# Longer bursts of the probability-value products in one part of an attention and Fourier-mixing kernel, with casts, loads and a transpose put elsewhere

## The chip, the core and the metric

The kernel runs on one core of a Trainium2 chip. The metric is device microseconds of the whole program. The engines are named as the profile names them: PE (TensorE, matmuls), PEld (its weight loads, which run beside the matmuls), DVE (VectorE), ACT (ScalarE), POOL (GpSimd) and SP (SyncE, which here only issues DMAs).

## What is computed

Two blocks over 2048 tokens of width 640 are mixed by a gate. Block A is attention with 32 heads of 20 elements; block B is a Fourier transform along the width and then along the sequence, of which the real part is kept.

```python
g = sigmoid((x * gate_w).sum(-1, keepdims=True))
q, k, v = split_heads(x @ wqkv)                  # 32 heads of 20
p = softmax(einsum("bhqd,bhkd->bhqk", q, k) * 20 ** -0.5)
a = merge_heads(einsum("bhqk,bhkd->bhqd", p, v)) @ wo
re, im = xB @ dft_hid_re.T, xB @ dft_hid_im.T
b = dft_seq_re @ re - dft_seq_im @ im
out = g * a + (1 - g) * b
```

All operands are fp32. A product that must be exact is made of three fp32r products of parts: an operand is cast to fp32r (its first part), and what the cast left out is its second part.

## The kernel before, in words

**Stages.** First come projections of q, k and v (lines 399 to 463). Then the attention runs for 1024 *steps*; beside it PE is given other matmuls as *fills*. There are 32 units (a pair of heads and half of the queries), each of 32 steps. The fills are, in this order: the rest of the Fourier transform along the width (the hidden part, 56 cycles), the transform along the sequence (the sequence part, 168 cycles), and the output projection (the output part, 32 cycles).

**A cycle** is four steps and follows a string of letters, `ORDERS` (lines 36 to 40):

- `e` is one score matmul (L907, 62 rows deep, 512 columns) with keys on the output's partitions. ACT turns it into probabilities by an exp (L909) into a tile `p`. There are 8 in a cycle.
- `m` is one score matmul (L187) with queries on the partitions, for a later unit, 41 steps ahead. DVE takes its maximum (L189). There are 8 in a cycle. When a unit's 64 maxima columns are there, DVE makes a negated maximum `nm` of them (L203), PE transposes it (L221), DVE splits the result into two fp32r parts (L114, L115), and SP writes them as two more rows beside q, so that the later `e` matmuls subtract the maximum.
- `F` is a place for fills. One fill of the sequence part (L608) is two matmuls of 64 rows and 320 columns, one on each half of the array's rows.
- `B` is the burst (function `burst`, L913): `av_step` for two key tiles. One key tile is four matmuls (L528), each of 21 output columns, on four column groups side by side, fp32, which the profile counts as two each. So a burst is 16 matmul records in four groups of four.

An `e` or `m` matmul uses half of the array's rows. The two tuples behind each string say which half comes first, so that both halves get the same work.

**Banks.** Of PSUM's eight banks, five (`ps0` to `ps4`) are taken in turn by scores and by the transpose, one is `av`, in which a unit's 16 key tiles are summed, and two are `yp0` and `yp1` for the fills. A score can't start before the bank of the score five places before it has been read. `av` is copied out by ACT at a unit's end (L536).

**What sets the order.** The program is written out by hand: each engine executes its instructions in the order in which this code calls them, and waits only for data and buffers. DMAs and slower steps hang on step numbers (`at_step`, `begin`).

**Operands of the sequence part.** Per 16 sequence tiles (48 fills, three cycles), two tiles `part` of Fourier coefficients are made: loaded by SP (L495), for some products summed of two (L501, POOL), cast (L114, POOL) and the remainder taken (L115, POOL). Of the transform along the width, 16 tiles `x` are made for each of seven products: loaded to `araw` (L512), for some products summed (L517, POOL), cast and subtracted on POOL (L114, L115). `run_extras` in the burst issues these, some bursts after the load. When 16 sequence tiles are done, ACT reads one half of the result (L627), DVE adds the other (L628), and POOL adds it to what was there (L742).

Of the kernel before, what the change touches and what calls it, by code (L numbers as in the profile page):

```python
# [75 lines left out]
def mix_kernel(ctx: ExitStack, tc: tile.TileContext, xa, wqk, wb, cdft, wo, out):  # L76
# [12 lines left out]
    ps_a = pools(name="ps_a", bufs=1, space=PSUM)  # L89
# [32 lines left out]
    turn = itertools.count()  # L122

    def bank():
        return ps_w.tile([P, 512], F32, name=f"ps{next(turn) % 5}")

    def pair_tile():
        return work.tile([P, 2, 512], F32, name="p", bufs=5)
# [4 lines left out]
    def part_tile():  # L133
        return work.tile([P, 2, 1024], R, name="part", bufs=3)

    def v_tile():
        return work.tile([P, NS, VW], F32, name="v", bufs=2)
# [102 lines left out]
    av = ps_a.tile([P, 512], F32, name="av")  # L240
    dve.memset(av, 0.0)
# [5 lines left out]
    def load_v(n):  # L247
# [5 lines left out]
        sp.dma_start(vts[n], v_scr[p])  # L253
# [10 lines left out]
    def load_first():  # L264
        wr, w = raw_tile()[:, : ND * P].rearrange("p (d c) -> p d c", d=ND), part_tile()
        w = w.rearrange("p z c -> p (z c)")[:, : 2 * ND * P].rearrange("p (z d c) -> p z d c", z=2, d=ND)
# [11 lines left out]
        split(w[:, 0, :1], w[:, 1, :1], wr[:, :1], act, dve)  # L278
        for d in range(ND):
            if d == 1:  # L280
                split(w[:, 0, 1:], w[:, 1, 1:], wr[:, 1:], act, dve)
            split(xs[0][:, 0, d], xs[0][:, 1, d], xr[d][1], act, dve)

    def load_wqk(c):
# [3 lines left out]
        def finish():  # L288
            w = part_tile().rearrange("p z c -> p (z c)")[:, : 2 * ND * P].rearrange("p (z d c) -> p z d c", z=2, d=ND)
            split(w[:, 0], w[:, 1], raw, act, dve)  # L290
# [26 lines left out]
    def qk_tile(c, t):  # L317
        w = wt[c]
        ps = bank()
        for d in range(ND):  # L320
            three(ps, w[:, 0, d], w[:, 1, d], xs[t][:, 0, d], xs[t][:, 1, d], d == 0, d == ND - 1)
# [13 lines left out]
    def v_pair(hf, s):  # L335
        vst = v_tile().rearrange("p s e -> p (s e)").rearrange("p (a k e) -> p a k e", a=NP // 2, k=2)
# [151 lines left out]
    def load_c(g):  # L488
# [9 lines left out]
        def finish():  # L498
            c = cparts[g] = part_tile()
            if len(raws) > 1:  # L500
                pool.tensor_tensor(raws[0], raws[0], raws[1], op=ALU.add if PRODUCTS[n][0][1][0] > 0 else ALU.subtract)  # L501
            split(c[:, 0], c[:, 1], raws[0], pool, pool)

        return finish

    def load_a(n, s):
# [7 lines left out]
        def finish():  # L514
            a = a_tile(n % 2, s)
            if len(raws) > 1:
                pool.tensor_tensor(raws[0], raws[0], raws[1], op=ALU.add if PRODUCTS[n][1][1][0] > 0 else ALU.subtract)  # L517
            split(a[:, 0], a[:, 1], raws[0], pool, pool)
# [531 lines left out]
```

## Time and profile before

Three runs took 1867.81, 1868.01 and 1868.48 us (median 1868.01 us). The profiled execution took 1869.47 us by the same clock; its span, from the first to the last instruction of the profile, was 1867.7 us, and shares and sums below go by this span.

| stage, us of the span | length | PE busy | DVE | ACT | POOL | DMA share |
|---|---|---|---|---|---|---|
| projections, 0 to 260 | 260 | 256.4 | 88.4 | 73.3 | 108.9 | 0.53 |
| hidden part, 260 to 606 | 346 | 345.7 | 277.4 | 276.7 | 98.3 | 0.28 |
| sequence part, 606 to 1668 | 1062 | 1062.0 | 891.2 | 768.0 | 853.4 | 0.58 |
| output part and tail, 1668 to 1868 | 200 | 194.3 | 126.7 | 154.1 | 102.0 | 0.28 |

The columns are the engines' busy time in each stage. A busy PE is one with a matmul in flight; several can be in flight at once, on different rows or columns of the array, so this column can't tell a dense stage from a loose one. What does is the distance in time from the start of one matmul to the next on the same half of the array. The granted TensorE clock was 0.99 to 1.00 in all four stages.

### The profile page before, as it was taken

What the parts mean: (1) busy time and instruction counts of PE and PEld (TensorE: products, weight loads), DVE (VectorE), ACT (ScalarE), POOL (GpSimd) and SP (SyncE); (2) the same over time, 40 slices, a digit from 0 to 9 for tenths busy, and PEclk for the clock granted to TensorE, in tenths of its full rate; (3) what the DMA queues carried; (4) which work ended last, traced back from release to release, by engine and by line L of the source; (5) the groups of instructions that cost most, each with busy time, mean ns of one, the idle gap of its engine ahead of it and who ended that gap; (6) DMA issues with size and microseconds to landing.
All of it is one profiled execution on the core that took longest, in us unless ns stands there. A gap on an engine that the chain in (4) does not pass through costs nothing.

```text
span 1867.7 us, 45004 instructions
## 1 busy us (share of the span) xinstructions
PE 1858.3 (100%) x17606; PEld 1360.8 (73%) x17606; DVE 1383.7 (74%) x2310; ACT 1272.1 (68%) x2439; POOL 1162.6 (62%) x1038
## 2 busy tenths in 40 slices
PE   9999999999999999999999999999999999999998
PEld 8988777676767777777777777767777777776666
DVE  3044458787878888888888888888888888888853
ACT  4222258787877777777777777777777777778885
POOL 3335432121146897466799899867779989635544
PEclk9999999999999999999999999999999999999999
DMA  6744341222134674535567576546476766431233
GB/s 230 174 136 151 139 127 56 78 65 68 54 99 139 209 209 142 161 128 175 185 192 241 163 249 191 176 140 179 145 240 203 214 198 202 142 90 47 88 98 108
DMA packets 178771, 281.61 MB, mean 151 GB/s; under 512 B 44811, under 2 KB 113547, under 8 KB 178559
## 3 DMA queue, kind: packets, MB, share of 16 engines
q1 hardware_dynamic: 177599, 276.77, 47.4%
q0 software_dynamic: 960, 1.97, 0.6%
q8 instruction: 138, 2.26, 0.5%
q14 instruction: 74, 0.61, 0.1%
HBM read 214.61 MB, written 63.52 MB: 149 GB/s over the span
## 4 chain that ended last, share of the span: by engine, by line
PE 98%; DMA 1%; POOL 0%; ACT 0%; DVE 0%; issue 0%; SPq 0%; POOLq 0%; ACTq 0%
PE av L528 25%; PE yp L608 19%; PE ps L907 16%; PE ps L187 15%; PE yp L363 7%; PE ps L118 4%; PE ps L120 4%; PE ps L119 4%; PE yp L715 3%; PE ps L221 0%; DMA p<-in_xa 0%; POOL p L115 0%; DMA a_scr<-raw 0%; DVE mx L189 0%; ACT p L323 0%
## 5 line engine op out<-in xcount | busy, mean ns | idle before, releaser
L189 DVE TENSOR_REDUCE mx<-ps 128x1 f32<-128x512 f32 x2048 | 1280.1, 684 | 298.9 <-PE ps L187 280.7
L909 ACT ACTIVATE p<-ps 128x512 f32<-128x512 f32 x2048 | 1109.1, 599 | 371.6 <-PE ps L187 248.9
L187 PE MATMUL ps<-kst,qst 60*128 60x512 f32 x1920 | 758.3, 410 | 0.0
L907 PE MATMUL ps<-qst,kst 62*128 62x512 f32 x1920 | 744.9, 407 | 0.1
L608 PE MATMUL yp<-x,part 64*128 64x320 f32 x5376 | 662.1, 306 | 0.3 <-ACT raw L373 0.3
L608 PEld LDWEIGHTS yp<-x,part 64*128 64x128 f32 x5376 | 624.7, 186 | 8.3 <-ACT raw L373 0.6
L528 PE MATMUL av<-p,v 128*21 128x512 f32 x4096 | 490.1, 596 | 0.0
L907 PEld LDWEIGHTS ps<-qst,kst 62*128 62x128 f32 x1920 | 348.1, 185 | 182.5 <-DVE mx L189 132.2
L187 PEld LDWEIGHTS ps<-kst,qst 60*128 60x128 f32 x1920 | 342.2, 184 | 7.9 <-issue 4.2
L115 POOL TENSOR_TENSOR part<-raw,part 128x1024 fp32r<-128x1024 f32 (+1 forms) x128 | 288.0, 2250 | 10.3
L528 PEld LDWEIGHTS av<-p,v 128*21 128x21 f32 x4096 | 97.6, 100 | 221.5 <-issue 218.3
L363 PE MATMUL yp<-wb,x 64*128 64x320 f32 x1920 | 224.0, 307 | 0.0
L374 POOL TENSOR_TENSOR raw<-raw 128x320 f32<-128x320 f32 x64 | 55.7, 870 | 268.4 <-ACT raw L373 219.1
L363 PEld LDWEIGHTS yp<-wb,x 64*128 64x128 f32 x1920 | 210.1, 186 | 6.0
L114 POOL CAST part<-raw 128x1024 fp32r<-128x1024 f32 (+1 forms) x128 | 126.1, 985 | 127.9 <-PE ps L187 67.0
L501 POOL TENSOR_TENSOR raw<-raw,raw 128x1024 f32<-128x1024 f32 x77 | 185.9, 2414 | 7.5 <-DMA raw<-in_cdft 6.0
L115 POOL TENSOR_TENSOR x<-araw,x 128x320 fp32r<-128x320 f32 x112 | 97.8, 873 | 9.0
L715 PE MATMUL yp<-x,part 64*128 64x320 f32 x768 | 102.2, 308 | 0.0
L323 ACT ACTIVATE p<-ps 128x512 f32<-128x512 f32 x40 | 23.8, 597 | 102.0 <-PE ps L120 85.5
L715 PEld LDWEIGHTS yp<-x,part 64*128 64x128 f32 x768 | 92.0, 186 | 1.0
L118 PE MATMUL ps<-x,part 128*128 128x512 f32 x200 | 80.7, 403 | 1.6 <-ACT x L112 1.3
L114 POOL CAST p<-p 128x512 fp32r<-128x512 f32 x40 | 24.7, 618 | 92.4 <-ACT p L323 92.4
(110 smaller groups left out, 1419.5 us busy)
## 6 DMA issues: line engine op xcount, KB each, us to landing
raw<-in_cdft SPq DMA_DIRECT2D x192, 512.0 KB
araw<-a_scr SPq DMA_DIRECT2D x192, 160.0 KB
qk_scr<-p SPq DMA_DIRECT2D x40, 512.0 KB
kst<-qk_scr SPq DMA_DIRECT2D x84, 160.0 KB
qst<-qk_scr SPq DMA_DIRECT2D x84, 160.0 KB
yt<-y_scr SPq DMA_DIRECT2D x80, 160.0 KB
a_scr<-raw SPq DMA_DIRECT2D x64, 160.0 KB
y_scr<-yt SPq DMA_DIRECT2D x64, 160.0 KB
```

What stands on the lines that cost most here:

```text
L114: e1.tensor_copy(dst1, src)
L115: e2.tensor_tensor(dst2, src, f32(dst1), op=ALU.subtract)
L118: pe.matmul(ps, st1, mv1, start=first, stop=False)
L187: pe.matmul(ps, q[b : b + KROWS, qt * P : (qt + 1) * P], k[b : b + KROWS, kc * 512 : (kc + 1) * 512], start=True, stop=True)
L189: return lambda: dve.tensor_reduce(mx[n][:, h, qt, kc : kc + 1], ps, axis=AX.X, op=ALU.max)
L363: pe.matmul(yp[h][:, :HE], x[r, xz, d, cs], w[r, wz, d, :HE], start=d == 0 and z == 0, stop=d == ND - 1 and z == 2)
L501: pool.tensor_tensor(raws[0], raws[0], raws[1], op=ALU.add if PRODUCTS[n][0][1][0] > 0 else ALU.subtract)
L528: pe.matmul(av[32 * j : 32 * j + DH + 1, :], v[:, kt, h * (DH + 1) : (h + 1) * (DH + 1)], pp[qc][:, h, :], start=kt == 0, stop=kt == NS - 1)
L608: pe.matmul(yp[h][:, :HE], c[r, cz, cs], a[r, az], start=s == 0 and z == 0, stop=s == NS - 1 and z == 2)
L715: pe.matmul(yp[h][:, :HE], o[oz][r], wos[d, hf][r, wz], start=d == 0 and z == 0, stop=end)
L907: pe.matmul(pt, k[b : b + KROWS + 2, kt * P : (kt + 1) * P], q[b : b + KROWS + 2, qc * 512 : (qc + 1) * 512], start=True, stop=True)
L909: act.activation(pts[n, kt, qc][:, h], pt, AF.Exp, scale=float(DH) ** -0.5)
```

## The change

In the sequence part alone, a cycle becomes six steps: 12 `e`, 12 `m`, 24 fills in 18 places, and a burst of three key tiles. So there are 112 cycles in place of 168; the hidden and the output part keep theirs. The new string packs the scores and the fills otherwise. With it come:

- 16 key tiles are no multiple of 3, so a unit can end inside a burst. Then the next unit takes another bank: all six banks are in one queue `places`, `av` is one of them, and `next_av` puts the old one at the queue's end. Scores still have five in turn.
- An `av` matmul is 32 columns wide in place of 21 (the 11 others reach into the next head's columns, and their results are not used), so each `v` tile has 16 zeroed columns behind it (POOL).
- The cast of `part` and of `x` goes from POOL to ACT in this part, and is issued by `run_casts` in the burst; the loads of `araw` and the sums of two are issued in the middle of the cycle (`run_loads`).
- The transpose of the maxima stands ahead of the burst's last key tile in this part; before, it stood behind the burst.
- Buffers: seven `p` tiles in place of five, two `part` tiles in place of three.

```diff
 ORDERS = (
     ("ememFFFeFFmeFFmFeFmFeFmFmFFeFemB", (0, 0, 1, 0), (1, 1, 0, 1)),
+    ("ememeFFFFmeFFemFeFmFemFeFeFmeFFmeFFFFmmemmB", (0, 0, 0, 1, 0, 1), (1, 1, 0, 1, 0, 0)),
+    ("emFeFmFeFFmFeFFmeFFmeFFmFmFeFmeB", (1, 0, 1, 1), (0, 1, 0, 0)),
     ("emFFeFmFeFFmFeFmFeFFmeFmFFmFemeB", (0, 1, 1, 0), (1, 0, 0, 1)),
-    ("emFeFmFeFFmFeFFmeFFmeFFmFmFeFmeB", (1, 0, 1, 1), (0, 1, 0, 0)),
 )
...
-    turn = itertools.count()
+    places = collections.deque(f"ps{k}" for k in range(6))
+
+    def place_tile(name):
+        return ps_w.tile([P, 512], F32, name=name)
 
     def bank():
-        return ps_w.tile([P, 512], F32, name=f"ps{next(turn) % 5}")
+        places.rotate(-1)
+        return place_tile(places[-1])
...
-    av = ps_a.tile([P, 512], F32, name="av")
-    dve.memset(av, 0.0)
+    av = {"name": places.pop()}
+
+    def next_av():
+        places.append(av["name"])
+        av["name"] = places.popleft()
+        av["tile"] = place_tile(av["name"])
+
+    av["tile"] = place_tile(av["name"])
...
-        def finish():
-            a = a_tile(n % 2, s)
+        def combine():
             if len(raws) > 1:
                 pool.tensor_tensor(raws[0], raws[0], raws[1], op=ALU.add if PRODUCTS[n][1][1][0] > 0 else ALU.subtract)
-            split(a[:, 0], a[:, 1], raws[0], pool, pool)
-
-        return finish
-
-    def av_step(i, n, kt):
+
+        def parts(e1):
+            a = a_tile(n % 2, s)
+            split(a[:, 0], a[:, 1], raws[0], e1, pool)
+
+        return combine, parts
+
+    def av_step(i, n, kt, split_unit):
         v = vts[n]
+        if split_unit:
+            next_av()
+        t, c0 = av["tile"], kt * VW
         pp = [pts.pop((n, kt, qc)) for qc in range(2)]
         for qc in range(2):
             for h in range(2):
                 j = 2 * qc + h
-                pe.matmul(av[32 * j : 32 * j + DH + 1, :], v[:, kt, h * (DH + 1) : (h + 1) * (DH + 1)],
+                pe.matmul(t[32 * j : 32 * j + 32, :], v[:, c0 + h * (DH + 1) : c0 + h * (DH + 1) + 32],
                           pp[qc][:, h, :], start=kt == 0, stop=kt == NS - 1)
...
-        if s % 8 == 4 and cfin and g // 8 + 2 < 2 * UNITS:
-            cfin.pop(0)()
+        if s % 8 == 2 and g // 8 + 2 < 2 * UNITS:
+            cfin[0][0]()
...
-        if more(g):
-            n = g // (HT * NS) + 1
-            preps.append(load_a(n, made.setdefault(n, 0)))
-            made[n] += 1
-        if len(preps) > 2 or preps and not more(g):
-            preps.pop(0)()
...
+    def run_casts():
+        if cfin and (done - HIDS) // 24 + 1 < 2 * UNITS:
+            cfin.pop(0)[1](act)
+        while preps["combined"]:
+            preps["combined"].pop(0)[1](act)
+
+    def run_loads(c):
+        while preps["loaded"]:
+            preps["combined"].append(preps["loaded"].pop(0))
+            preps["combined"][-1][0]()
+        n = c // (2 * HT) + 1
+        if n < len(PRODUCTS):
+            k = made.get(n, 0)
+            made[n] = min(NS, k + 1 + (c % 4 == 3))
+            preps["loaded"].extend(load_a(n, s) for s in range(k, made[n]))
...
-        edge.append(edge[-1] + 3)
+        edge.append(edge[-1] + 2)
...
     def burst(c):
         for n in ends:
             max_nm(n)
-        run_extras(max(done - HIDS, 0) // 3, 2)
-        for kt in (2 * c, 2 * c + 1):
-            av_step(now[0], kt // NS, kt % NS)
+        k, _, i = phase(c)
+        steps = 6 if k == 1 else 4
+        run_extras(steps - 2)
+        if k == 1:
+            run_casts()
+        for kt in range(i // 2, (i + steps) // 2):
+            if k == 1 and ends and kt == (i + steps) // 2 - 1:
+                max_chain(ends.pop(0))
+            av_step(now[0], kt // NS, kt % NS, kt % NS == 0 and kt > i // 2)
         while ends:
             max_chain(ends.pop(0))
...
+            if k == 1 and x == len(order) // 2:
+                run_loads(c - HID)
```

PE's order around a burst of the sequence part that has a transpose. Before, from the last fill of a cycle to the first fill of the next (L608 is a fill, L907 an `e`, L187 an `m`, L528 the burst, L221 the transpose):

```order
L608 MATMUL yp_17233<-x_14678,part 128x320
L608 MATMUL yp_17234<-x_14678,part 128x320
L907 MATMUL ps_17423<-qst_91,kst_89 128x512
L187 MATMUL ps_17426<-kst_90,qst_92 128x512
L907 MATMUL ps_17429<-qst_91,kst_89 128x512
L528 MATMUL av<-p,v 21x512 x8
L221 MATMUL ps_17449<-ident,nm 16x128
L907 MATMUL ps_17456<-qst_91,kst_89 128x512
L187 MATMUL ps_17459<-kst_90,qst_92 128x512
L608 MATMUL yp_17233<-x_14678,part 128x320
```

The same place with the change, from the cycle's last scores (L950 is an `e`, L197 an `m`, L556 the burst, L231 the transpose, and `ps_16895` is the bank that serves as `av`):

```order
L197 MATMUL ps_17366<-kst_87,qst_89 128x512
L950 MATMUL ps_17369<-qst_88,kst_86 128x512
L197 MATMUL ps_17372<-kst_87,qst_89 128x512
L197 MATMUL ps_17375<-kst_87,qst_89 128x512
L556 MATMUL ps_16895<-p,v 32x512 x8
L231 MATMUL ps_17398<-ident,nm 16x128
L556 MATMUL ps_16895<-p,v 32x512 x4
L950 MATMUL ps_17409<-qst_88,kst_86 128x512
L197 MATMUL ps_17413<-kst_87,qst_89 128x512
L950 MATMUL ps_17416<-qst_88,kst_86 128x512
L197 MATMUL ps_17419<-kst_87,qst_89 128x512
L950 MATMUL ps_17427<-qst_88,kst_86 128x512
```

The transpose has moved from behind the burst to between its second and third key tile; before, `e`, `m`, `e` stood last ahead of a burst and two scores behind it ahead of the next fill; now `m`, `m`, `e`, `m`, `m` stand ahead (the first of them just above these rows) and five scores behind.

ACT's order around a burst of the sequence part, before (L909 is an exp, L627 the read of a fills' result):

```order
L909 ACTIVATE p<-ps_14895 128x512
L909 ACTIVATE p<-ps_14901 128x512
L627 ACTIVATE m<-yp_14586 128x320
L909 ACTIVATE p<-ps_14922 128x512
L909 ACTIVATE p<-ps_14938 128x512
```

and with the change (L952 is an exp, L113 a cast):

```order
L952 ACTIVATE p<-ps_17348 128x512
L952 ACTIVATE p<-ps_17369 128x512
L113 ACTIVATE part<-raw 128x1024
L113 ACTIVATE x_17385<-araw 128x320 x2
L952 ACTIVATE p<-ps_17409 128x512
L952 ACTIVATE p<-ps_17416 128x512
```

One cast of a whole `part` and one or two of an `x` tile now stand between the last exp of a cycle and the first of the next.

More of the change, by code (lines that the diff above doesn't have):

```diff
@@ L133, in part_tile, with w_tiles @@
     def part_tile():
-        return work.tile([P, 2, 1024], R, name="part", bufs=3)
+        return work.tile([P, 2, 1024], R, name="part", bufs=2)
+    def w_tiles():
+        w = part_tile()
+        return [w[:, z, : ND * P].rearrange("p (d c) -> p d c", d=ND) for z in range(2)]
     def v_tile():
-        return work.tile([P, NS, VW], F32, name="v", bufs=2)
+        return work.tile([P, NS * VW + 16], F32, name="v", bufs=2)
     def load_part(t, o, p, parts, blocks):
@@ L807, in mix_kernel @@
             share = count * (c + 1 - c0) // (c1 - c0) - count * (c - c0) // (c1 - c0)
-            places = order_of(c)[0].count("F")
-            goals[c] = [at_goal + share * (f + 1) // places for f in range(places)]
+            fills_ = order_of(c)[0].count("F")
+            goals[c] = [at_goal + share * (f + 1) // fills_ for f in range(fills_)]
             at_goal += share
@@ L953, in take @@
             pool.tensor_tensor(y, y, m, op=ALU.add)
-    ring = itertools.cycle([(ps_w, f"ps{k}") for k in range(5)] + [(ps_a, "av"), (ps_y, "yp0"), (ps_y, "yp1")])
+    ring = itertools.cycle([(ps_w, name) for name in (*places, av["name"])] + [(ps_y, "yp0"), (ps_y, "yp1")])
     def free_bank():
```

83 lines of the change are left out of this document (47 added, 36 removed).

## The prediction

> **What bounds the kernel now.** I read the page first, then the timeline of PE in the sequence part, then DVE's, ACT's and POOL's rows against it.
>
> ```profile
> span 1867.7 us, 45004 instructions
> PE 98%; DMA 1%; POOL 0%; ACT 0%; DVE 0%; issue 0%; SPq 0%; POOLq 0%; ACTq 0%
> ```
>
> The second line is the chain that ended last, by engine: PE is all of it. So only what makes PE's starts lie farther apart or closer counts. One whole cycle of the sequence part in the timeline (start, duration, engine, line, output<-inputs, count):
>
> ```profile
> 904.71 1.92 PE L528 MATMUL av<-p,v 128*21 128x512 f32 x16
> 905.16 0.12 PEld L528 LDWEIGHTS av<-p,v 128*21 128x21 f32 x4 [0.31 <-issue]
> 905.59 0.12 PEld L528 LDWEIGHTS av<-p,v 128*21 128x21 f32 x4 [0.31 <-issue]
> 906.56 0.50 PE L907 MATMUL ps<-qst,kst 62*128 62x512 f32 x1
> 906.56 0.50 PE L187 MATMUL ps<-kst,qst 60*128 60x512 f32 x1
> 906.90 0.60 PE L608 MATMUL yp<-x,part 64*128 64x320 f32 x5
> 907.20 0.40 PE L907 MATMUL ps<-qst,kst 62*128 62x512 f32 x1
> 907.34 0.39 PE L187 MATMUL ps<-kst,qst 60*128 60x512 f32 x1
> 907.44 0.31 PE L608 MATMUL yp<-x,part 64*128 64x320 f32 x1
> ...
> 910.68 0.39 PE L907 MATMUL ps<-qst,kst 62*128 62x512 f32 x1
> 911.00 1.91 PE L528 MATMUL av<-p,v 128*21 128x512 f32 x16
> ```
>
> A cycle is 911.00 - 904.71 = 6.29 us: a burst of 906.56 - 904.71 = 1.85 and a stretch of scores and fills of 911.00 - 906.56 = 4.44. A score holds its half of the array for 907.44 - 907.20 = 0.24 us (the fill at 907.44 follows the `e` at 907.20 on the same half; the `m` at 907.34 runs on the other). With eight scores and sixteen fills for each half, and 0.18 of edges (below), a fill takes (4.44 - 0.18 - 8 x 0.235) / 16 = 0.148. A group of four burst matmuls takes 905.59 - 905.16 = 0.43.
>
> **Fewer changes between bursts and scores: a gain.** Three edges of a cycle cost more than the work in it. The first two scores hold their halves 906.90 - 906.56 = 0.34, which is 0.10 over 0.24. The last score's start and the burst's lie 911.00 - 910.68 = 0.32 apart, 0.08 over. The burst's four groups are 1.72 of its 1.85, 0.13 over. That is 0.31 us for a cycle, however long its burst. Twelve scores and 24 fills on each half and six groups are exactly one and a half times the old contents, so the new cycle would last 1.5 x (6.29 - 0.31) + 0.31 = 9.28 us. With 112 in place of 168, 56 x 0.31 = **-17.4 us**.
>
> **The transpose ahead of the last key tile: a loss.** DVE makes `nm` behind all maxima of the cycle. How that stands to PE in a burst of before:
>
> ```profile
> 891.96 1.91 PE L528 MATMUL av<-p,v 128*21 128x512 f32 x16
> 892.44 0.68 DVE L189 TENSOR_REDUCE mx<-ps 128x1 f32<-128x512 f32 x1
> 893.04 0.21 DVE L203 TENSOR_REDUCE nm<-mx 128x16 f32<-128x64 f32 x1
> 893.80 0.28 PE L221 MATMUL ps<-ident,nm 128*16 128x128 f32 x1
> 894.01 0.50 PE L907 MATMUL ps<-qst,kst 62*128 62x512 f32 x1
> ...
> 907.13 5.06 DVE L189 TENSOR_REDUCE mx<-ps 128x1 f32<-128x512 f32 x8 [0.56 <-PE ps L187]
> L221 PE MATMUL ps<-ident,nm 128*16 128x128 f32 x21 | 5.8, 277 | 0.0
> ```
>
> `nm` is there at 893.04 + 0.21 = 893.25, 1.29 behind the burst's start; PE comes to the transpose at 893.80, 1.84 behind it. So nobody waits, and the transpose costs 894.01 - 891.96 = 2.05 less 1.85 = 0.20. After the change PE is at the transpose after two key tiles again, thus at 1.84, but DVE is later. The string ends in `m m e m m`: by 0.235 for each score on a half, and 0.32 for the last, these four `m` start 0.79, 0.55, 0.32 and 0.32 ahead of the burst. A reduction starts 0.47 behind its score (907.13 against the `m` of 906.56, less the 0.10 of a first pair) and the next 0.60 later (893.04 - 892.44). So DVE starts them at -0.32, 0.28, 0.88 and 1.48 from the burst's start, `nm` at 2.08, and has it at 2.29. PE waits 2.29 + 0.05 - 1.84 = 0.50. Besides, PE drains ahead of the transpose (893.80 is 0.12 more than four groups behind 891.96), spends 894.01 - 893.80 = 0.21 on it, and only then does the last key tile. That is 0.8 for a transpose, 0.6 more than before, in 21 bursts of this part (the count in the last row): **+12.8 us**. Below, with no wait, this is 21 x 0.1 = 2; above, with 0.2 more for a DVE that also ends late, 17. I take the worked value. What is queued behind the wait is the burst's last key tile and all scores of the next cycle; ACT and DVE then run empty, which gives nothing back.
>
> **Packed scores and five banks: a loss.** A score needs the bank of the score five places before it. In the output part before, fills are few and scores dense:
>
> ```profile
> 321.64 0.63 PE L528 MATMUL av<-p,v 128*21 128x512 f32 x4
> 327.81 0.63 PE L528 MATMUL av<-p,v 128*21 128x512 f32 x4
> ...
> 1680.23 0.63 PE L528 MATMUL av<-p,v 128*21 128x512 f32 x4
> 1686.23 0.63 PE L528 MATMUL av<-p,v 128*21 128x512 f32 x4
> 1688.66 0.60 ACT L909 ACTIVATE p<-ps 128x512 f32<-128x512 f32 x1 [0.81 <-PE ps L187]
> 1689.32 0.18 PEld L187 LDWEIGHTS ps<-kst,qst 60*128 60x128 f32 x1
> 1689.32 0.49 PE L187 MATMUL ps<-kst,qst 60*128 60x512 f32 x1
> ```
>
> There the exp ends at 1689.26, the weights of the score that gets its bank load 0.06 later, and the score lasts 0.49 in place of 0.39: a bank comes back 0.16 behind its reader's end. A cycle there has twelve fills: 12 x 0.148 + 8 x 0.235 + 0.31 + 1.72 = 5.69, but the starts lie 1686.23 - 1680.23 = 6.00 apart; the banks cost 0.31. In the hidden part (fifteen fills, the first two rows) it is 6.17 against 6.13, 0.04. In the sequence part it is nothing. By scores that is 0.229 us of work for each score in the output part, 0.256 in the hidden part, 0.266 in the sequence part (fills and scores of a half, over sixteen). The new string has 0.266 as a mean, but between its two clumps of fills fourteen scores share thirteen fills: 7 x 0.235 + 13 x 0.148 = 3.57, which is 0.255, the hidden part's density. That gives 14/16 of 0.04, and the sixth score, behind five at once and five fills, adds some 0.03: its bank's exp starts 0.57 and ends 1.17 behind the cycle's start, so it is back at 1.33, and its half is free at 0.34 + 0.235 + 5 x 0.148 = 1.31. I take 0.07 for a cycle, **+7.8 us**; the bounds are 0 and the output part's 0.31 x 24/16 = 0.47, so 0 to 52 us. It is nearest to the hidden part.
>
> **32 columns for 21: a small loss.** A weight load grows with its columns:
>
> ```profile
> L907 PEld LDWEIGHTS ps<-qst,kst 62*128 62x128 f32 x1920 | 348.1, 185 | 182.5 <-DVE mx L189 132.2
> L528 PEld LDWEIGHTS av<-p,v 128*21 128x21 f32 x4096 | 97.6, 100 | 221.5 <-issue 218.3
> ```
>
> That is (185 - 100) / 107 = 0.8 ns for a column, 9 ns for eleven. Only the first load of a burst lies open (the 0.08 ahead of it is about its length); the others run under the group before. 200 bursts x 9 ns: **+1.8 us**, bounds 0 and 2.
>
> **Casts on ACT, loads and sums in mid-cycle, buffers: nothing.** What hides them is a whole cycle: a `part` is cast a cycle ahead of its first fill, an `x` up to sixteen cycles. POOL loses the two casts and gets the small memset of `v` for each new pair of heads. Without that cover each late tile would stop PE for its lateness. What ACT must not do is hold the exps up:
>
> ```profile
> 904.62 1.09 ACT L909 ACTIVATE p<-ps 128x512 f32<-128x512 f32 x2 [0.39 <-PE yp L608]
> 905.60 0.44 ACT L627 ACTIVATE m<-yp 128x320 f32<-128x320 f32 x1
> L112 ACT ACTIVATE x<-raw 128x1024 fp32r<-128x1024 f32 x6 | 6.4, 1062 | 9.3 <-DMA raw<-in_xa 9.3
> L112 ACT ACTIVATE x<-raw 128x512 fp32r<-128x512 f32 x4 | 2.5, 623 | 2.1 <-DMA raw<-in_xa 2.1
> L112 ACT ACTIVATE p<-o 128x256 fp32r<-128x256 f32 x2 | 0.8, 418 | 1.2 <-DVE o L1006 1.2
> ```
>
> Two exps take 1.09, so the second adds 0.49 to 0.60. The new string's last `e` starts 0.55 ahead of the burst and its exp ends some 0.5 behind the burst's start; the next cycle's first exp is due 0.6 behind its first score, that is 2.58 + 0.13 + 0.6 = 3.3 behind. In these 2.8 us stand one cast of 1024 columns (1.06), one or two of 320 (0.42 to 0.62 each by the rows, I take 0.47), and at times the read (0.44) or the copy of `av` (as long as an exp, 0.60): 1.5 to 2.6. It fits, so I take nothing; below there is no gain, since PE waited for none of POOL's casts; above it is the second rival.
>
> **Sum.** -17.4 + 12.8 + 7.8 + 1.8 = +5.0 us on the profiled span of 1867.7. The median of the runs, 1868.0, is within 0.3 of that span, so I add the sum to it: **1873 us**, slower by 0.27%. The two large losses are each less sure than the gain; the likeliest case's own range is 1869 to 1879.
>
> **Rivals.**
>
> *The gain comes through (faster).* If `nm` is there when PE comes, and the banks keep up, what is left is -17.4 + 2 + 1.8 = -13.6: **1854 us**. For it: in every burst shown DVE was done 0.55 ahead of PE. Against: that was with one `m` in the last 0.5 us ahead of the burst, not three. Chance 0.22.
>
> *ACT's casts hold the exps up (slower).* The cast of `x` waits for POOL's sum, issued in mid-cycle, and ACT can't pass it. Such a stop exists in the trace, where the hidden part ends:
>
> ```profile
> 602.57 0.50 PE L907 MATMUL ps<-qst,kst 62*128 62x512 f32 x1
> 602.89 0.77 ACT L373 ACTIVATE raw<-yp 128x320 f32<-128x320 f32 x2 [1.32 <-DMA a_scr<-raw]
> 604.02 0.62 ACT L909 ACTIVATE p<-ps 128x512 f32<-128x512 f32 x1
> ...
> L115 POOL TENSOR_TENSOR part<-raw,part 128x1024 fp32r<-128x1024 f32 x110 | 262.6, 2388 | 8.8
> L501 POOL TENSOR_TENSOR raw<-raw,raw 128x1024 f32<-128x1024 f32 x77 | 185.9, 2414 | 7.5 <-DMA raw<-in_cdft 6.0 <-PE ps L187 1.5
> L517 POOL TENSOR_TENSOR araw<-araw 128x320 f32<-128x320 f32 x80 | 69.9, 874 | 0.7 <-DMA araw<-a_scr 0.7
> ```
>
> ACT waited for a DMA, and an exp came 604.02 - 602.57 = 1.45 behind its score in place of 0.6. The Trainium skill, "PSUM — Partial Sum Buffer", section "Engine vs sequencer instructions", states that ScalarE's queue is strict FIFO; that is this rival's rule, and these rows agree with it. POOL's work in a cycle with all sums is 2.39 + 2.41, two to four of 0.87 for `x`, and on average one more of that shape for a result: 9.2 at most against 9.35, and 7.6 on average with five tiles `x` in four cycles. So for some cycles the sum for `x` ends close to ACT's turn. It decides from 0.3 us of lateness on; with 0.2 us lost in each cycle the forecast rises by 112 x 0.2 = 22 to **1895 us**. Chance 0.16.
>
> *It cancels.* With the transpose's wait as worked out and no loss at the banks: -17.4 + 12.8 + 1.8 = -2.8, **1865 us**; that the casts and loads do nothing at all is part of this and of the forecast. Chance 0.14.
>
> **How the numbers follow.** The forecast has 0.48, the rivals 0.22, 0.16 and 0.14. What a measurement can't tell from no change is 0.2%, 3.7 us. Faster than that is the first rival and a little of the third: 0.24. Within it are most of the third and the forecast's lower end (1869 to 1871.7): 0.18. Slower are the rest of the forecast and the second rival: 0.58. The range, 1854 to 1892, holds all but the far half of each outer rival.
>
> **What will show it.** In the sequence part, bursts start some 9.35 us apart: 9.28 would say that the banks cost nothing, 9.5 that they cost more. Burst edges stay at 0.34, 0.32 and 0.13. In bursts with a transpose, `nm` ends 2.3 us behind the burst's start and PE starts the transpose right behind it, the cycle being 0.8 longer; a transpose at 1.84 refutes that step. First exps behind a burst that start over 0.7 behind their score would mean the second rival, as would PE waiting on ACT with a cast ahead. A wait of PE for `part` or `x` would refute the cover.

## The result, and the profile after

The changed kernel took 1879.03 us (median of 4 runs, 1877.31 to 1881.32) against 1867.91 before: a ratio of 1.006, 95% interval 1.0042 to 1.0077. The forecast was 1873, slower. Two of the versions below had one run each of another length, 8134.42 and 3615.46 us, which their ratios leave out. The profiled execution has a span of 1877.5 us against 1867.7, so 9.8 us are to be found. The page, its first line and the chain that ended last, by engine:

```profile
span 1877.5 us, 44813 instructions
PE 95%; DVE 3%; issue 0%; DMA 0%; POOL 0%; ACT 0%; SPq 0%; POOLq 0%; ACTq 0%; DVEq 0%
```

The chain was 98% PE and 0% DVE before; now 3% of it is DVE, some 56 us. In each burst of the sequence part that has a transpose the chain leaves PE for the last four maxima and `nm` (2.6 us around the burst at 641.24). That is the length of DVE's pieces in the chain and not PE's idle time, which is shown below. In the same profile the distances between bursts tell in which stage the time came: to the first burst +2.0 us, hidden part +1.0, sequence part to the first output burst +6.2, output part +0.7, tail -0.1. One plain cycle of the sequence part, PE's timeline of the changed kernel (start, duration, engine, line, operation):

```profile
765.02 0.43 PE L197 MATMUL ps<-kst,qst 60*128 60x512 f32 x2
765.38 2.78 PE L556 MATMUL ps<-p,v 128*32 128x512 f32 x24
768.09 0.50 PE L950 MATMUL ps<-qst,kst 62*128 62x512 f32 x1
768.09 0.73 PE L197 MATMUL ps<-kst,qst 60*128 60x512 f32 x2
768.43 0.63 PE L950 MATMUL ps<-qst,kst 62*128 62x512 f32 x2
...
774.71 2.78 PE L556 MATMUL ps<-p,v 128*32 128x512 f32 x24
```

The cycle is 774.71 - 765.38 = 9.33 long (median of the 90 plain cycles 9.344, forecast 9.35). The burst is 768.09 - 765.38 = 2.71, which is six groups of 0.43 and the same 0.13 as before; the first pair of scores holds its halves 768.43 - 768.09 = 0.34, again as before. So an edge costs what it cost, and there are fewer of them. The third edge is unchanged too: the last score's start and the burst's lie 0.32 apart (median in both kernels). A burst with a transpose, all engines:

```profile
641.24 1.92 PE L556 MATMUL ps<-p,v 128*32 128x512 f32 x16
...
643.28 0.21 DVE L213 TENSOR_REDUCE nm<-mx 128x16 f32<-128x64 f32 x1
643.54 0.09 PEld L231 LDWEIGHTS ps<-ident,nm 128*16 128x16 f32 x1 [1.29 <-DVE nm L213]
643.55 0.28 PE L231 MATMUL ps<-ident,nm 128*16 128x128 f32 x1 [0.38 <-DVE nm L213]
643.75 1.06 PE L556 MATMUL ps<-p,v 128*32 128x512 f32 x8
644.75 0.50 PE L950 MATMUL ps<-qst,kst 62*128 62x512 f32 x1
...
651.38 1.07 PE L556 MATMUL ps<-p,v 128*32 128x512 f32 x8
```

`nm` ends 643.28 + 0.21 - 641.24 = 2.25 behind the burst's start (forecast 2.29), the transpose starts at 2.31, and the cycle lasts 651.38 - 641.24 = 10.14. In 14 of the 21 such bursts it is so; in the other seven `nm` ends at 2.38 to 2.41, and the cycle is 0.1 to 0.2 longer still. The table of waits of PE's matmuls in this kernel (who, for whom: us in all, times, longest), its first row and one that the kernel before does not have:

```profile
PE ps L231 <- DVE nm L213: 9.3, 22, 0.5
...
PE ps L197 <- ACT p L952: 1.2, 1, 1.2
```

The first row stands 22 times in the profile where the kernel before has one such wait of 0.4. The second is a single event, late in the sequence part; POOL, ACT and PE of the changed kernel around it:

```profile
1588.09 0.46 POOL L115 CAST x<-raw 128x320 fp32r<-128x320 f32 x1 [4.21 <-DMA raw<-in_wo]
...
1594.01 2.38 POOL L516 TENSOR_TENSOR raw<-raw,raw 128x1024 f32<-128x1024 f32 x1
1596.42 1.06 ACT L113 ACTIVATE part<-raw 128x1024 fp32r<-128x1024 f32 x1 [3.23 <-POOL raw L516]
1597.39 5.47 ACT L952 ACTIVATE p<-ps 128x512 f32<-128x512 f32 x11
1598.02 0.50 PE L197 MATMUL ps<-x 60*128 60x512 f32 x1 [1.21 <-ACT p L952]
```

POOL stood 4.21 us for a load of output weights, so its sum for `part` came late; ACT stood 3.23 us in front of the cast of `part`, the exps queued behind it, and the score that needed a bank of theirs started 1.21 late. The cycle is 1.6 longer than its like. That is the mechanism of the second rival (it named the cast of `x`, here it is that of `part`), in one cycle of 112. The Trainium skill, "PSUM — Partial Sum Buffer", section "Engine vs sequencer instructions", calls ScalarE's queue strict FIFO, and these rows agree.

The five banks can be seen in the plain cycle above. Its sixth score takes the bank of its first `e`; ACT reads that one, and the score's weights follow:

```profile
768.69 0.60 ACT L952 ACTIVATE p<-ps 128x512 f32<-128x512 f32 x1 [1.89 <-PE ps L197]
...
769.34 0.18 PEld L197 LDWEIGHTS ps<-kst,qst 60*128 60x128 f32 x1
```

The exp ends at 769.29, and the weights load 0.05 behind it, as they do in the median of the plain cycles. So this score waits for its bank, where the forecast put a loss.

### The profile page after: what moved, and what is told of

Its sections match the earlier page's. It is cut to its first block, busy times and chain, and to the rows that moved or that the text cites. A ratio compares the mean times of both kernels' runs of the same rounds, so it can differ in the third digit from the quotient of the medians.

```text
span 1877.5 us, 44813 instructions
## 1 busy us (share of the span) xinstructions
PE 1858.4 (99%) x17606; PEld 1372.2 (73%) x17606; DVE 1380.5 (74%) x2309; ACT 1355.7 (72%) x2645; POOL 1002.0 (53%) x851
## 4 chain that ended last, share of the span: by engine, by line
PE 95%; DVE 3%; issue 0%; DMA 0%; POOL 0%; ACT 0%; SPq 0%; POOLq 0%; ACTq 0%; DVEq 0%
PE ps L556 23%; PE yp L636 19%; PE ps L950 17%; PE ps L197 14%; PE yp L379 7%; PE ps L119 4%; PE ps L120 4%; PE ps L121 4%; PE yp L743 3%; DVE mx L199 3%; PE ps L231 0%; DMA p<-in_xa 0%; DVE nm L213 0%; PE ps L1037 0%; POOL raw L516 0%
## 5 line engine op out<-in xcount | busy, mean ns | idle before, releaser
L952 ACT ACTIVATE p<-ps 128x512 f32<-128x512 f32 x2048 | 1054.1, 611 | 298.9 <-PE ps L197 193.8
L950 PE MATMUL ps<-qst,kst 62*128 62x512 f32 x1920 | 728.2, 407 | 0.1
L197 PE MATMUL ps<-kst,qst 60*128 60x512 f32 x1920 | 668.1, 411 | 0.0
L636 PE MATMUL yp<-x,part 64*128 64x320 f32 x5376 | 629.2, 307 | 0.0
L636 PEld LDWEIGHTS yp<-x,part 64*128 64x128 f32 x5376 | 606.0, 186 | 5.8 <-ACT raw L389 0.4
L556 PE MATMUL ps<-p,v 128*32 128x512 f32 x4096 | 485.3, 597 | 0.0
L116 POOL TENSOR_TENSOR part<-raw,part 128x1024 fp32r<-128x1024 f32 (+1 forms) x128 | 287.2, 2244 | 345.2 <-ACT part L113 329.5
L950 PEld LDWEIGHTS ps<-qst,kst 62*128 62x128 f32 x1920 | 341.7, 185 | 155.0 <-DVE mx L199 85.5
L197 PEld LDWEIGHTS ps<-kst,qst 60*128 60x128 f32 x1920 | 318.7, 184 | 12.5 <-issue 4.2
L556 PEld LDWEIGHTS ps<-p,v 128*32 128x32 f32 x4096 | 110.8, 109 | 233.0 <-issue 225.1
L113 ACT ACTIVATE part<-raw 128x1024 fp32r<-128x1024 f32 (+2 forms) x121 | 123.4, 1020 | 6.0 <-POOL raw L516 4.1
L743 PE MATMUL yp<-x,part 64*128 64x320 f32 x768 | 102.6, 309 | 0.0
L339 ACT ACTIVATE p<-ps 128x512 f32<-128x512 f32 x40 | 23.8, 597 | 104.1 <-PE ps L121 101.1
L116 POOL TENSOR_TENSOR x<-araw,x 128x320 fp32r<-128x320 f32 x112 | 97.9, 882 | 1.3
L743 PEld LDWEIGHTS yp<-x,part 64*128 64x128 f32 x768 | 92.0, 186 | 1.0
L119 PE MATMUL ps<-x,part 128*128 128x512 f32 x200 | 81.4, 407 | 1.5 <-ACT x L113 1.3
L120 PE MATMUL ps<-x,part 128*128 128x512 f32 x200 | 80.0, 400 | 0.2 <-DVE x L116 0.2
```

The source lines that it names most:

```text
L116: e2.tensor_tensor(dst2, src, f32(dst1), op=ALU.subtract)
L119: pe.matmul(ps, st1, mv1, start=first, stop=False)
L120: pe.matmul(ps, st1, mv2, start=False, stop=False)
L197: pe.matmul(ps, q[b : b + KROWS, qt * P : (qt + 1) * P], k[b : b + KROWS, kc * 512 : (kc + 1) * 512], start=True, stop=True)
L556: pe.matmul(t[32 * j : 32 * j + 32, :], v[:, c0 + h * (DH + 1) : c0 + h * (DH + 1) + 32], pp[qc][:, h, :], start=kt == 0, stop=kt == NS - 1)
L636: pe.matmul(yp[h][:, :HE], c[r, cz, cs], a[r, az], start=s == 0 and z == 0, stop=s == NS - 1 and z == 2)
```

## The experiments

Each comparison is with runs of the kernel before on the same chip, whose median there stands behind the word before.

**The transpose behind the burst again.**

```diff
-            if k == 1 and ends and kt == (i + steps) // 2 - 1:
-                max_chain(ends.pop(0))
             av_step(now[0], kt // NS, kt % NS, kt % NS == 0 and kt > i // 2)
```

> The changed kernel with the transpose back behind the burst's last key tile. Theory (in the 21 bursts of the sequence part that carry one, PE stands for the negated maxima, which end 2.29 us behind the burst's start, while a third key tile is still to do): PE comes to the transpose at 2.70, waits for nothing, and such a cycle is 0.2 longer than a plain one instead of 0.8 to 0.9; 21 x 0.63 = 13 us less, about 1866 us. Rival 1 (the early transpose buys time for the rows that the next unit's scores read): scores wait at the head of a unit, the time stays at 1879 or rises. Rival 2 (the cost is the drain and the transpose itself, not the wait): cycles stay 0.8 longer, 1879.

Measured: 1874.5 us (1868.37 to 1884.14), before 1868.67, ratio 1.0032 (1.0018 to 1.0047). Timeline of this kernel:

```profile
639.14 2.78 PE L556 MATMUL ps<-p,v 128*32 128x512 f32 x24
...
641.85 0.28 PE L231 MATMUL ps<-ident,nm 128*16 128x128 f32 x1
...
642.81 0.18 PEld L950 LDWEIGHTS ps<-qst,kst 62*128 62x128 f32 x1 [0.45 <-DVE m L116]
...
648.95 2.78 PE L556 MATMUL ps<-p,v 128*32 128x512 f32 x24
```

The wait for `nm` is gone: PE's table of waits has it once, 0.4 us, as before the change. But the cycle is 648.95 - 639.14 = 9.81, 0.48 over a plain one (9.33) and not 0.2, and the median lies 8 us above the 1866 of the expectation: the string opens with five scores, the transpose has just taken one of the five free banks, and the fifth score stands 0.45 for DVE's `m` (L116), the second read of the transpose. So the wait was real, and behind it stood a bank. The profiled run had, besides, two plain cycles that were 4.5 and 5.2 us longer than the rest. In the first DVE stood for a small load:

```profile
1082.97 0.25 DVE L578 RECIPROCAL lc<-lc 128x16 f32<-128x16 f32 x1 [2.98 <-DMA lc<-l_scr]
```

The maxima queued behind it, and PE waited 2.7 for one of them. The second is the event of the output weights, this time with ACT 5.30 idle in front of its cast. The 16 us between the fastest and the slowest run of this kernel would take several such events; one run alone was profiled, so that they make the spread is not shown.

**32 columns in the kernel before, and the tiles' places.** The changed `v` is 16 columns longer and there are two buffers, so all that lies behind it moves by 2 x 16 x 4 = 128 bytes in each partition: the tiles `x` and a buffer of `wb`.

```diff
-        return work.tile([P, NS, VW], F32, name="v", bufs=2)
+        return work.tile([P, NS * VW + 16], F32, name="v", bufs=2)
-                pe.matmul(av[32 * j : 32 * j + DH + 1, :], v[:, kt, h * (DH + 1) : (h + 1) * (DH + 1)],
+                pe.matmul(av[32 * j : 32 * j + 32, :], v[:, kt * VW + h * (DH + 1) : kt * VW + h * (DH + 1) + 32],
```

> The kernel before with 32 columns in place of 21 in each weight load of the bursts, and the tile v 16 columns longer. Theory: only the first load of each of 256 bursts is open, 9 to 10 ns each: 2.4 us more, about 1870.3. Rival 1 (all loads are hidden): 1867.9. Rival 2 (all sixteen loads of a burst count): 4096 x 9 ns = 37 us more. Rival 3 (the longer tile shifts the tiles behind it, and that is what made the projections slower after the change): projections' matmuls 1.5 ns farther apart, 2.0 us more at the start, 1872.

Measured: 1876.03 us (1875.82 to 1876.54), before 1868.67, ratio 1.0037 (1.0025 to 1.0049): more than any of the expectations but the second rival's. A burst is 1.855 in place of 1.845, as the theory has it. Beside it the projections' matmuls stood some 233 ns apart in place of 229 (third rival), and a stretch of scores and fills in the sequence part grew by 25 ns. So the next run moved the tiles without touching the matmuls.

```diff
-        return work.tile([P, NS, VW], F32, name="v", bufs=2)
+        return work.tile([P, NS * VW + 16], F32, name="v", bufs=2)[:, : NS * VW].rearrange("p (s e) -> p s e", s=NS)
```

> The kernel before with each tile v 16 columns longer (two buffers, so 128 bytes more in each partition ahead of the tiles x), and nothing else: no instruction reads those columns. Theory (the place of x, not the 32 columns, slows the matmuls that move x): projections' matmuls 195.0 ns apart on average in place of 193.0 (scores between them left in), first burst 2 us later than it would be; in the sequence part a stretch of scores and fills 4.466 in place of 4.441, the burst at 1.845; 2 + 168 x 0.025 + 1 = 7 less the burst loads' 2.4 that the version with 32 columns had: about 1873.5. Rival (the 32 columns did all of it): as before, 1868.5.

Measured: 1873.55 us (1872.01 to 1877.47 but for the one long run), before 1869.11, ratio 1.0023 (1.0012 to 1.0034). Two tiles of the projections in PE's timeline, first and thirtieth matmul; the kernel before, then this one:

```profile
148.34 0.50 PE L118 MATMUL ps<-x,part 128*128 128x512 f32 x1
...
155.10 0.39 PE L120 MATMUL ps<-x,part 128*128 128x512 f32 x1
```

```profile
150.63 0.50 PE L118 MATMUL ps<-x,part 128*128 128x512 f32 x1
...
157.50 0.40 PE L120 MATMUL ps<-x,part 128*128 128x512 f32 x1
```

155.10 - 148.34 = 6.76 against 157.50 - 150.63 = 6.87: 0.11 for 30 matmuls, 2.2 us for the 600 of the projections. No instruction differs. In the sequence part a stretch is 4.448 (median) in place of 4.441, not 4.466: that part of the run with 32 columns, some 18 ns for each of 168 cycles, does not come from the place, and its cause was not found. Of the 4.4 us between the medians, 2.2 and 168 x 0.007 = 1.2 are placed so. The profiled run, the slowest of the six at 1877.47 us, waited besides 3.3 us in place of 1.3 for the first `x` of the projections.

Back on the changed kernel, the tiles moved by another 128 bytes (`NS * VW + 32`):

> The changed kernel with each tile v 16 columns longer still, so that all tiles behind lie 256 bytes and not 128 behind their old places. Theory (128 bytes off a boundary of 256): projections' spacing back at 193.0, first burst 2 us sooner, a plain stretch of the sequence part 6.61 less 24 x 1.5 ns = 6.577, burst still 2.713; -2.0 - 4.1 - 0.8 gives 1872. Rival (any shift does it, or it is a drift of the chip): 1879, stretch 6.61 to 6.63.

```profile
149.15 0.50 PE L119 MATMUL ps<-x,part 128*128 128x512 f32 x1
...
155.91 0.39 PE L121 MATMUL ps<-x,part 128*128 128x512 f32 x1
```

6.76 again. The same two rows of the changed kernel:

```profile
149.07 0.50 PE L119 MATMUL ps<-x,part 128*128 128x512 f32 x1
...
155.94 0.40 PE L121 MATMUL ps<-x,part 128*128 128x512 f32 x1
```

There it is 155.94 - 149.07 = 6.87. So the place of `x` decides the pace of the matmuls that move it, and 256 bytes do no harm where 128 do: in all seven profiles with the tiles 128 bytes farther the projections' matmuls stand 233 ns apart, in the seven with them at the old place or 256 bytes farther 229 or 230. The stretch went only from 6.630 to 6.608, not to 6.577; four other profiles with the changed string and 128 bytes have 6.614 to 6.617, so fills suffer next to nothing of it. The time, 1879.33 us (1874.38 to 1879.79; before 1869.11, ratio 1.005, 1.0037 to 1.0063), is not the 1872 of the theory and shows no gain beyond the spread of 5 us: the profiled run has one cycle of 5.1 us too much, again that of the output weights.

The weights' second part next to the first instead of at a stride of 1024:

```diff
-        return [w[:, z, : ND * P].rearrange("p (d c) -> p d c", d=ND) for z in range(2)]
+        w = w.rearrange("p z c -> p (z c)")
+        return [w[:, z * ND * P : (z + 1) * ND * P].rearrange("p (d c) -> p d c", d=ND) for z in range(2)]
```

> The changed kernel with the two parts of a projection weight next to each other again (the second 640 columns behind the first in place of 1024). Theory: the start is 2.0 us longer after the change because the projections' matmuls, 600 of them, are 233 ns apart in place of 229, and the place of the weight's second part is the cause: spacing back at 229, first burst 2.0 us sooner, 1877.0. Rival: the place of the weights does nothing, spacing stays at 233, 1879.0; then another shift of the tiles, or the run itself, is the cause.

Measured: 1879.79 us (1875.14 to 1881.38), before 1868.67, ratio 1.0053 (1.0041 to 1.0066); spacing unchanged at 233 ns. The rival holds: where the weights' second part lies makes no difference.

**The casts on POOL again** (`parts(act)` in the burst becomes `parts(pool)`).

> The changed kernel with the casts of the sequence part on POOL again, in the same places of the order. Theory (a whole cycle covers them on either engine): POOL is busy about 62% in place of 53%, PE waits for nothing, 1879 within 1.5. Rival 1 (ACT's casts hold exps up and so lengthen cycles): plain cycles go from 9.34 towards 9.28, about 1873. Rival 2 (POOL is too slow for all of it in cycles with both sums): PE waits for part or x, over 1885.

Measured: 1881.02 us (1879.42 to 1881.6), before 1868.67, ratio 1.006 (1.0047 to 1.0073), plain cycles 9.330, POOL busy 61%. The median is 0.5 over the theory's upper bound, and the ratio is that of the changed kernel. In the step asked for the theory holds: on either engine the casts cost nothing in a plain cycle (9.328 in the run before this one, which has them on ACT). The run also tells how the load of the output weights reaches PE. POOL stood 3.33 us for it here too, but in the sequence part PE waits for ACT nowhere: without casts on ACT, that lateness did not get to the exps. The long cycle at this place (1.95 over the others) is another load's, that of the sums, for which the reciprocal on DVE stood 1.34.

**The best of both, as a test of the bank.** Tiles at 256 bytes, the transpose behind the burst, and the fifth score behind a fill:

```diff
-    ("ememeFFFFmeFFemFeFmFemFeFeFmeFFmeFFFFmmemmB", (0, 0, 0, 1, 0, 1), (1, 1, 0, 1, 0, 0)),
+    ("ememFeFFFmeFFemFeFmFemFeFeFmeFFmeFFFFmmemmB", (0, 0, 0, 1, 0, 1), (1, 1, 0, 1, 0, 0)),
```

> Tiles moved by 256 bytes as in the run beside it; the transpose behind the burst; and the fifth score of the string behind one fill (ememFeFFF for ememeFFFF), since with the transpose behind the burst that score stood 0.45 us for the bank of the transpose. Theory: a cycle with a transpose is 0.21 longer than a plain one (0.48 when only the transpose was moved, 0.79 to 0.92 after the change): 21 x 0.6 = 12.6 below the aligned run, about 1859.5, plus what late loads of single runs cost (0 to 9). Rival 1 (the bank of the transpose is late for the fills behind as well): 0.48 stays, 1865. Rival 2 (the string with the later score costs the plain cycles as much): plain stretch over 6.60.

Measured: 1862.41 us (1859.6 to 1865.16), before 1869.11, ratio 0.9963 (0.9951 to 0.9976). A cycle with a transpose is 0.34 over a plain one, between the theory's 0.21 and the first rival's 0.48. Then the two late loads were given more time as well:

```diff
-        steps = (6, 10, 16, 23, 27, 34, 45) if n < NU - 4 else (1, 4, 7, 8, 11, 14, 16)
+        steps = (6, 10, 20, 25, 29, 36, 45) if n < NU - 4 else (1, 4, 7, 8, 11, 14, 16)
-            if r == 5 and d < ND:
+            if r == 7 and d < ND:
```

> The version beside it, with the reciprocal of the sums 4 steps later behind its load (and the three steps behind it 2 later), and the output weights' parts made two steps later behind their load. Theory: two single stalls, of DVE for the load of the sums (3.0 us in one cycle of an earlier run) and of POOL for the output weights (6.1 us in another, by which ACT's cast, the exps and PE came late), make the spread of 1868 to 1884 between runs of one kernel: here the spread shrinks to 2 us, and the median lies 1 to 5 below the run beside it. Rival (other loads come late as well): the same median and spread.

Measured: 1859.03 us (1857.4 to 1861.85), before 1869.11, ratio 0.9951 (0.9938 to 0.9965). This is faster than both kernels. The edit moves three steps behind the reciprocal as well, by two steps each. Its timeline:

```profile
635.86 2.78 PE L556 MATMUL ps<-p,v 128*32 128x512 f32 x24
638.58 0.28 PE L231 MATMUL ps<-ident,nm 128*16 128x128 f32 x1
...
639.54 0.18 PEld L950 LDWEIGHTS ps<-qst,kst 62*128 62x128 f32 x1 [0.22 <-DVE m L116]
...
645.52 1.07 PE L556 MATMUL ps<-p,v 128*32 128x512 f32 x8
```

A cycle with a transpose is 645.52 - 635.86 = 9.66, 0.35 over its plain ones (9.312): one fill ahead of the fifth score took half of the stand of 0.45 away, so the forecast of 0.21 was missed by the other half. The spread did not shrink to 2 us, but the median fell by 3.4.

**The late loads alone**, on the changed kernel:

> The changed kernel with only the two late loads given more time: the reciprocal 4 steps later behind its load, the output weights' parts 2 steps later behind theirs. Theory: 20 plain cycles that now last 0.08 to 0.1 longer (the reciprocal stands between two maxima in the densest place) become like the others, 1.8 us less, and the single stalls of up to 5 us go; 1875 to 1877, spread 2 us. Rival: the 0.08 comes from something else that recurs once per unit, 1879 and the same spread.

Measured: 1875.58 us (1872.99 to 1876.61), before 1868.5, ratio 1.0029 (1.0019 to 1.004). The median is as forecast, the spread of 3.6 us is not. In the changed kernel 20 plain cycles, one for each unit that ends, are 0.06 to 0.08 longer than the rest. DVE there:

```profile
684.76 1.29 DVE L199 TENSOR_REDUCE mx<-ps 128x1 f32<-128x512 f32 x2 [0.18 <-PE ps L197]
685.96 0.24 DVE L578 RECIPROCAL lc<-lc 128x16 f32<-128x16 f32 x1
686.12 1.93 DVE L199 TENSOR_REDUCE mx<-ps 128x1 f32<-128x512 f32 x3
```

The reciprocal stands between maxima without a gap, so those behind it, and the banks they read, come later. In the run with other steps those 20 cycles are like the others (two further ones are off, by 0.24 and 1.7). The event of the output weights is still there, with 1.7 us: POOL stood 4.24 for the load, so two steps more were not enough in this run.

The same edit in the kernel before:

> The kernel before with the two loads given more time, as in the versions of the changed one (reciprocal 4 steps later, output weights' parts 2 steps later). Theory (the reciprocal costs PE something only between the packed scores and fills of the new string, and only the new order lets a late load reach PE by ACT's casts): the kernel before gains nothing, 1868 to 1869. Rival (the kernel before had the same losses, and the changed one only shares them): 2 to 3 us less, 1865.5.

Measured: 1866.98 us (1865.77 to 1870.02), before 1867.85, ratio 0.9998 (0.9989 to 1.0007). No gain beyond the interval, and in the profile of the kernel before no plain cycle of the sequence part stands out by more than 0.26: these losses came with the change.

**Maxima that end early, with the transpose left where the change puts it.** Tiles at 256 bytes, late loads, and the old string one and a half times:

```diff
-    ("ememeFFFFmeFFemFeFmFemFeFeFmeFFmeFFFFmmemmB", (0, 0, 0, 1, 0, 1), (1, 1, 0, 1, 0, 0)),
+    ("emFFeFmFeFFmFeFmemFFeFmFeFFmFeFmFeFFmeFmFFmFemeB", (0, 1, 0, 1, 1, 0), (1, 0, 1, 0, 0, 1)),
```

> Tiles moved by 256 bytes, the two loads given more time, and the kernel before's string of scores and fills instead of the packed one: its first half, its first half again, its second half. The transpose stays ahead of the burst's last key tile. Theory (what made the transpose dear is that four maxima come in the last 0.8 us ahead of the burst; here they end as before): the negated maxima are there some 1.3 us behind the burst's start, PE comes to the transpose at 1.84 and waits for nothing, and such a cycle is 0.2 to 0.35 longer than a plain one in place of 0.8; a plain cycle is 9.28 to 9.30 if the packed scores cost something at the banks; about 1856. Rival 1 (being inside the burst costs by itself, wait or none): 0.6 and more over a plain cycle, 1863. Rival 2 (the packed string is not the worse one at the banks): plain cycles of 9.31 to 9.36, 1858 to 1863.

Measured: 1872.75 us (1870.65 to 1875.87), before 1868.5, ratio 1.0021 (1.0013 to 1.003); the theory's 1856 was missed by 17 us. Timeline:

```profile
639.47 1.92 PE L556 MATMUL ps<-p,v 128*32 128x512 f32 x16
640.68 0.21 DVE L213 TENSOR_REDUCE nm<-mx 128x16 f32<-128x64 f32 x1
...
641.33 0.28 PE L231 MATMUL ps<-ident,nm 128*16 128x128 f32 x1
641.54 1.06 PE L556 MATMUL ps<-p,v 128*32 128x512 f32 x8
...
649.26 2.78 PE L556 MATMUL ps<-p,v 128*32 128x512 f32 x24
658.69 1.49 PE L556 MATMUL ps<-p,v 128*32 128x512 f32 x12
```

Here `nm` is there 1.42 behind the burst's start, the transpose starts at 641.33 - 639.47 = 1.86 with no wait, and the cycle is 649.26 - 639.47 = 9.79, 0.36 over a plain one of 658.69 - 649.26 = 9.43. So the maxima's lateness made 0.8 out of 0.36. But the plain cycles are 0.13 longer than the packed string's (9.438 against 9.312), 14 us for 112. The second rival has the direction, and its 9.31 to 9.36 was too little. One and a half old cycles are 1.5 x 6.286 = 9.43 us, so with this string the longer burst gained nothing. Its edges are as short as before (0.34, 0.33 and 0.13), so the 0.15 beyond 9.28 and the loads' 0.01 stands between them. By PE's starts, each matmul given to its half in the order of the program (16 plain cycles), over half of it is at the seam where the half string is repeated (`m e m` in a row): scores there hold their halves 0.08 to 0.10 longer. What they wait for was not found, so that the packed string is better at the banks in general is not shown.

> The version beside it with the transpose behind the burst. Theory: the same plain cycles; a cycle with a transpose 0.21 longer than a plain one, so 21 x 0.1 = 2 us below the version beside it, about 1854. Rival (the transpose's bank is missed by the scores behind it, as in the run that moved the transpose alone, 0.48): 3 us above it.

Measured: 1869.6 us (1868.05 to 1871.82 but for the one long run), before 1868.5, ratio 1.0004 (0.9995 to 1.0013). A cycle with a transpose is 9.667, 0.23 over a plain one of 9.439. For the transpose the theory holds, 3 us below the run beside it; its 1854 fell with the plain cycles.

## Why the prediction was right, and what it missed

The direction and the two large terms were right. But 9.8 us stand in the profile, and 11 between the medians, where 5.0 were worked out: the time lies at the very end of the likeliest case's range (1869 to 1879). That it is well inside the full range, 1854 to 1892, is owed to the room left for the second rival, which did not come in every cycle; this much is luck.

| term, us | forecast | measured in the profile |
|---|---|---|
| fewer edges | -17.4 | -17.4 (same 0.31 in each cycle, 56 fewer) |
| transpose ahead of the last key tile | +12.8 | +13.0: 21 cycles, 0.83 over the plain median, less 0.21 before |
| banks | +7.8 | +6.0, what is left of a plain cycle: 112 x (9.344 - 9.28 - 0.01) |
| 32 columns | +1.8 | +2.0: 0.010 in each of 200 bursts |
| tiles 128 bytes farther | 0 | +2.2 in the projections |
| reciprocal between packed maxima | 0 | +1.6 |
| ACT behind late sums, two cycles | 0 | +1.3 (1.62 and 0.23, less 0.55 of single long cycles before) |

That makes 8.7; 1.1 us, spread over the hidden, sequence and output parts, is not placed.

*Edges.* Right: 0.34, 0.32 and 0.13 are the same before and after. In the kernel before, with each matmul given to its half, nothing but the edges is lost in a plain cycle: between them scores hold 0.235 and fills 0.148 throughout. The price of an edge was not changed by itself in any run. Against the kernel before, plain cycles gained 112 x (1.5 x 6.286 - 9.344) = 9.5 us net of what follows; with the old string repeated they gained nothing.

*Transpose.* Right, place and price: `nm` at 2.25 in most bursts instead of 2.29, and the runs that took the wait away (behind the burst; maxima that end early) both show it gone. One step was incomplete: "below, with no wait, this is 21 x 0.1" had the cost without a wait at 0.3 for a transpose; it measured 0.36 inside the burst, and behind it 0.48 with this string, since the bank that the transpose takes is missed by the fifth of the packed scores. The prediction asked for the wait of PE, and not for the bank.

*Banks.* Nearly the right size (0.054 for a cycle where 0.07 was taken), and at the sixth score the mechanism is seen: 0.05 behind its bank's reader, 0.03 to 0.05 longer on its half. The rest of the row is a remainder and less sure. Four other profiles with this string have plain cycles of 9.327 to 9.330, which would make it 4 us; and a part can belong to the 32 columns, which in the kernel before lengthened the stretches for a reason that was not found. The other term, taken over from the hidden part's density, was a guess by likeness. The upper bound, 0.47, was far.

*32 columns.* Right in the burst: 109 ns for a load in place of 100. In the kernel before the same edit cost 7.4 us by the medians, of which the place of the tiles and the bursts explain some 4.6 (2.2, and 256 x 9.5 ns); the other 3 are the 18 ns in each stretch whose cause is open.

*Casts, loads, buffers at nothing.* This is the step that failed, and it failed by what rode along. The casts did cost nothing in a plain cycle, as moving them back showed. "Buffers ... nothing" missed that a longer `v` moves `x`: +2.2. "Loads and sums in mid-cycle ... nothing" missed that a reciprocal on DVE and, by the casts on ACT, a late load now reach PE: +1.6 and +1.3, and up to 5 us in single cycles of other runs. The second rival had the latter's mechanism; its price of 0.2 in every cycle was wrong, it is a rare event of microseconds. (POOL's 7.6 us on average is 7.8 by its own terms, which changes nothing.)

*The first rival* named the gain that is there: the version with the transpose behind the burst, a fill ahead of the fifth score, tiles at 256 bytes and later steps is 10.1 us faster than the kernel before on its chip, where the rival has 13.6. *The third* has -2.8 where 9.8 were measured: 6.0 of that are the banks it left out, 5.1 the three terms that nobody had.

## What to carry to other kernels

When a burst is made longer and its surroundings denser, ask of each instruction that stays in the dense place (a transpose, a reciprocal, a small load's first use) what queue and what bank it now holds up; here that ate the whole gain, and moving these, one score and the tiles by a little made the same change a gain of 0.5%. Ask what a tile that grows does to the places of all tiles behind it. And look at the longest cycles, not at the median alone: loads that land late showed up as cycles 2 to 5 us too long in one profile and not in the next.

## What the runs showed of the hardware that was not expected

The matmuls that move 512 fp32r columns of `x` came 0.11 us in 30 later (some 233 ns apart in place of 229) when `x` lay 128 bytes farther in its partitions, and at the old pace when it lay 256 bytes farther; the place of the weights' second part made no difference. Whether it is the read of the moving operand, and which boundary counts, was not tried beyond these two distances.
